# Six GpSimd steps of a fused attention and channel-mix kernel wait for a VectorE step

## The chip, the cores and the metric

One core of one Trainium2 chip runs the kernel. The metric is the device time of one execution in microseconds (us). Inside the core five engines work side by side: TensorE (PE, the matmuls; its weight loads are listed as PEld), VectorE (DVE), ScalarE (ACT), GpSimd (POOL), and SyncE (SP), which here only issues DMAs. Each engine works through its own queue in program order; an instruction starts when the ones ahead of it are through and the semaphores that it waits for have come.

## The reference

The inputs q, k and v are 4 batches x 4 heads x 1088 positions x 32 numbers. The first part is an attention with polynomial features, linear in the sequence:

```
def phi(x):
    a = np.einsum('rd,bhsd->bhsr', S1, x)
    b = np.einsum('rd,bhsd->bhsr', S2, x)
    return np.einsum('bhsi,bhsj->bhsij', a, b).reshape(*x.shape[:-1], r * r)
q_p, k_p = (phi(q), phi(k))
kv = np.einsum('bhsf,bhsd->bhfd', k_p, v)
z = np.sum(k_p, axis=2)
num = np.einsum('bhsf,bhfd->bhsd', q_p, kv)
den = np.einsum('bhsf,bhf->bhs', q_p, z)[..., None] + 1e-06
```

Its result num / den, with the heads side by side, is x (4 x 1088 x 128). The second part mixes each position with the one before it and runs a two-layer network with a gate:

```
xk = mu_k * x + (1.0 - mu_k) * x_prev
xr = mu_r * x + (1.0 - mu_r) * x_prev
k = np.maximum(xk @ w_k, 0.0)
v = k * k @ w_v
r = 1.0 / (1.0 + np.exp(-(xr @ w_r)))
return (r * v).astype(np.float32)
```

Here r = 8 features each (64 products), and the inner width of the network is 1024.

## The kernel before

The kernel is a set of small functions, each of which issues one step of the work, and a string, `ORDER`, in which the steps are written out by hand in the order in which they are issued. The loop at lines 622 to 628 takes the entries one after the other. An entry such as `qp.2.0.V` names the function (`qp`), its arguments (batch 2, half 0) and the engine (V VectorE, G GpSimd, A ScalarE; P also means VectorE, with an operand read in PSUM); `@` gives the PSUM banks. Entries without an engine letter are TensorE steps, except those whose function fixes the engine. Since each engine works in order, `ORDER` fixes the queue of every engine. Waits between engines are put in by the framework, from the tiles that a step reads and writes and from the buffers that it takes over; two steps on different engines that share no tile are free to run at the same time.

The work of one batch, in the names that the prediction uses (lines are those of the step's instruction; many copies go through the helper `copy`, lines 200 and 202):

- Attention, key side: `turn` (L259, L262) transposes k and q in 32x32 blocks on VectorE; `kproj` projects on TensorE, `abev` copies the result out, `kp` (L296) forms the 64 products, `kvmm` (L325) multiplies them with v, `kvev` copies out (tile kvs), `kvt` (L343) transposes on TensorE, `kvtev` copies out.
- Attention, query side: `abw` (L384) projects q, `abwev` copies out; `pw` (L404) and `den` (L411, L412) form the denominator; `an` (L420) divides one factor by it; `qp` (L429) forms the 64 products of each position, 128x1152 in half 0 and 128x1024 in half 1, both inputs from SBUF when the letter is V or G; `qd` (L438) transposes them on VectorE; `xmm` (L511) and `xt` (L477) multiply with kv; `xev` and `xtev` copy x out, and `xs` copies 31 numbers per row so that each position finds the one before it.
- Channel mix, on groups g of 512 columns of positions (g = 2 x batch + half; g = 8 holds the 64 left over of every batch row): `xk` (L527) and `xkt` (L530) mix on VectorE with one input in PSUM; `f1.g.c` (L551) is the first layer, c one quarter of the inner width; `relu` (L559) on ScalarE writes k1; `sq` (L574) squares it into k2 (128x1024 bf16, both inputs the same SBUF tile); `f2.g.c` (L584) is the second layer, summed over c. `xh` and `xht` cast x to bf16 for the gate: `rr` (L597) multiplies, `sig` (L605) takes the sigmoid on ScalarE, `fin` (L610) multiplies gate and result on VectorE and issues the output DMAs. `wset` (L208) and `cset` prepare weights, `zz` (L173) are matmuls on zeros.

PSUM has eight banks, handed out in `ORDER`; a TensorE step also waits until the reader of what stood in its bank before is through. So `f1.5.0@12` waits for `fin.2`, which reads `f2.2`'s sums in bank 2, and `xmm.3.2@4567` for `relu.4.2` (banks 5 and 6).

Of the kernel before, what the change touches and what calls it, by code (L numbers as in the profile page):

```python
# [34 lines left out]
ORDER = """  # L35
turn.k.0.0.V smm.0@0 cset.0 turn.k.0.1.V zz.5@7 kproj.0.1@0 abev.0.1.A kproj.0.0@1 turn.q.0.1.V cset.4.G abev.0.0.V
smm.1@2 cset.1.V cset.2.G turn.q.0.0.V kp.0.0.G zz.1@7 zmm.0@3 zev.0.A zz.2@7 wmm.0 wsq.0 kp.0.1.P zz.2@7 abw.0.0@2
abwev.0.0.A pw.0.0.P den.0.0 an.0.0.V abw.0.1@3 abwev.0.1.A pw.0.1.G kvmm.0@2 kvev.0.A zz.2@7 kvt.0 turn.k.1.2.V
zz.3@7 kproj.1.1@0 den.0.1 qp.0.0.G an.0.1.G qp.0.1.P abev.1.1.A kp.1.1.G kproj.1.0@1 abev.1.0.A kvtev.0.A qt.0.0@45
qtev.0.0.A turn.q.1.2.V wset.0.G qtt.0@2 qt.0.1@67 qttev.0.A zmm.1@3 zev.1.A qtev.0.1.A zz.2@5 wmm.1 xmm.0.0@45 xt.0  # L40
xtev.0.A xev.0.0.A xmm.0.1@67 kp.1.0.P xev.0.1.A wsq.1 abw.1.1@3 cset.3 xs.0.V xk.0.0 xh.0.0.A xk.0.1 xh.0.1.A
abw.1.0@1 abwev.1.1.V xkt.0 abwev.1.0.A f1.0.3@45 wset.2.G relu.0.3.A f1.0.0@67 wset.1.G relu.0.0.A pw.1.2.G f1.1.3@23
f1.1.2@01 rr.0@4 sig.0.A relu.1.2.A relu.1.3.A turn.k.2.2.V kproj.2.1@5 den.1.2 kproj.2.0@6 abev.2.0.A turn.q.2.2.V
f1.1.0@01 kvmm.1@4 abev.2.1.V zmm.2@2 turn.k.3.2.V kproj.3.0@3 kp.2.0.P kproj.3.1@5 relu.1.0.A zev.2.A wmm.2 f1.0.1@01
sq.0.0.A kvev.1.A kvt.1 abev.3.1.V abev.3.0.A sq.0.3.G relu.0.1.A wsq.2 f1.0.2@67 relu.0.2.A abw.2.0@3 an.1.2.G
qp.1.0.G qp.1.1.G kvtev.1.A rr.1@0 qd.1.0.V qd.1.1.V sig.1.A sq.0.1.A abwev.2.0.V abw.2.1@1 abwev.2.1.A xmm.1.2@4567
turn.q.3.2.V kp.3.1.G zmm.3@3 xt.1@1 xev.1.1.V sq.0.2.A xtev.1.V kp.3.0.G zev.3.V f2.0.0@0 f2.0.1 xev.1.0.A wmm.3
xs.1.G sq.1.2.A f2.0.2 sq.1.3.A xkt.1 f2.0.3 xk.1.0 pw.2.2.G xk.1.1 f1.1.1@12 relu.1.1.A f1.2.0@45 relu.2.0.A wsq.3
fin.0.S f1.3.1@67 den.2.2 sq.1.1.V an.2.2.V abw.3.0@0 abw.3.1@1 relu.3.1.A f1.3.2@23 f1.2.1@45 sq.2.0.A sq.1.0.V
relu.2.1.A xht.0.G kp.2.1.G kvmm.2@6 kvmm.3@7 abwev.3.0.A qp.2.0.V sq.3.1.V xh.1.0.G kvev.2.V qp.2.1.G abwev.3.1.V  # L50
kvev.3.V kvt.2 relu.3.2.A f1.3.0@45 relu.3.0.A pw.3.2.G qd.2.0.V qd.2.1.V f1.3.3@01 relu.3.3.A kvtev.2.V sq.3.0.V
f2.1.0@2 f2.1.1 kvt.3 kvtev.3.A f1.2.3@34 relu.2.3.A sq.2.3.V xh.1.1.G f2.1.2 den.3.2 f1.2.2@01 relu.2.2.A f2.1.3
sq.3.2.A xmm.2.2@3456 xev.2.0.A sq.2.1.G xt.2@0 fin.1.S rr.2@1 xtev.2.V xs.2.G xh.2.0.G an.3.2.G f2.3.0@7 xev.2.1.V
sq.2.2.A sig.2.A xk.2.0 xkt.2 xk.2.1 qp.3.0.V f2.2.0@2 qd.3.0.V f2.3.1 f2.2.1 f1.4.0@01 f2.2.2 f1.4.1@34 sq.3.3.A
relu.4.0.A f2.2.3 fin.2.S relu.4.1.A f1.4.3@56 relu.4.3.A qp.3.1.G sq.4.0.G rr.3@0 sig.3.A f1.5.3@34 f2.3.2 f2.3.3
f1.4.2@56 qd.3.1.V relu.5.3.A fin.3.S sq.4.3.V relu.4.2.A sq.4.2.V f1.5.0@12 sq.4.1.V rr.4@0 sig.4.A xt.3@3 xh.2.1.V
xtev.3.A sq.5.3.V xs.3.V relu.5.0.A sq.5.0.G xmm.3.2@4567 f2.4.0@0 xev.3.0.A xev.3.1.A xkt.3 f1.5.1@12 f2.4.1 f2.4.2
xk.3.0 xk.3.1 rr.5@3 xht.3.V relu.5.1.A sig.5.A f1.5.2@12 sq.5.1.V f2.4.3 xh.3.0.V relu.5.2.A sq.5.2.V f1.6.3@45
relu.6.3.A fin.4.S xh.3.1.V f2.5.0@3 f1.6.0@67 f2.5.1 sq.6.3.V relu.6.0.A f1.6.1@12 relu.6.1.A f2.5.2 f1.6.2@45
relu.6.2.A f2.5.3 f1.7.1@67 relu.7.1.A sq.6.0.V fin.5.S sq.6.1.V sq.6.2.V f1.7.0@01 relu.7.0.A sq.7.0.V f2.6.0@2  # L60
xht.1.V sq.7.1.V f1.8.0@45 relu.8.0.A rr.7@3 f2.6.1 f1.7.3@67 relu.7.3.A sq.7.3.V sq.8.0.V f2.6.2 f1.7.2@01 relu.7.2.A
f2.6.3 sq.7.2.V f1.8.1@45 relu.8.1.A rr.6@6 sig.6.A f2.7.0@7 f1.8.3@01 relu.8.3.A f2.7.1 sq.8.1.V f1.8.2@45 relu.8.2.A
f2.7.2 sig.7.A f2.7.3 xht.2.G rr.8@0 fin.6.S sq.8.3.V sig.8.A sq.8.2.V f2.8.0@4 f2.8.1 fin.7.S f2.8.2 f2.8.3 fin.8.SAG
"""


# [592 lines left out]
```

## Time and profile before

| | us |
|---|---|
| median of 3 runs | 87.15 |
| fastest and slowest of them | 86.06, 87.16 |
| the profiled execution | 86.39 |
| its span in the profile | 84.6 |

In the rows that the prediction shows, the first number is the start in us from the begin of the span, the second the duration in us; then come the engine, the line, the operation, the tiles written and read, the shapes, the number of instructions merged in the row (x1, x2), and in brackets how long the engine had stood idle before the row and what it had waited for. An instruction on VectorE is listed from about 0.07 us before the one ahead of it ends, so starts lie closer than durations. The span in 40 slices of 2.1 us, busy tenths of each:

```profile
PE   5989999999999989999985999997985999999200
DVE  5269677896999899389999999999999999699400
ACT  0602041488999997699991999999764699999000
POOL 5032949899399999288642842997084000000300
PEclk9999999999999999999999999999999999999995
```

The granted TensorE clock is at 9 tenths or more until the last slice. GpSimd has work mainly in the first three quarters; VectorE and TensorE are listed as busy almost throughout, and a step that has started and is held up is listed as busy.

### The profile page before, as it was taken

What the parts mean: (1) busy time and instruction counts of PE and PEld (TensorE: products, weight loads), DVE (VectorE), ACT (ScalarE), POOL (GpSimd) and SP (SyncE); (2) the same over time, 40 slices, a digit from 0 to 9 for tenths busy, and PEclk for the clock granted to TensorE, in tenths of its full rate; (3) what the DMA queues carried; (4) which work ended last, traced back from release to release, by engine and by line L of the source; (5) the groups of instructions that cost most, each with busy time, mean ns of one, the idle gap of its engine ahead of it and who ended that gap; (6) DMA issues with size and microseconds to landing.
All of it is one profiled execution on the core that took longest, in us unless ns stands there. A gap on an engine that the chain in (4) does not pass through costs nothing.

```text
span 84.6 us, 3600 instructions
## 1 busy us (share of the span) xinstructions
PE 73.8 (87%) x1558; PEld 54.1 (64%) x1558; DVE 69.7 (82%) x121; ACT 58.7 (69%) x87; POOL 44.5 (53%) x54
## 2 busy tenths in 40 slices
PE   5989999999999989999985999997985999999200
PEld 2257786977598857496673879674644777899100
DVE  5269677896999899389999999999999999699400
ACT  0602041488999997699991999999764699999000
POOL 5032949899399999288642842997084000000300
PEclk9999999999999999999999999999999999999995
DMA  0999999999999600001210000400350004400550
GB/s 1 285 313 246 348 385 226 277 366 354 337 197 231 156 1 8 8 0 31 74 31 8 0 8 0 124 12 0 95 143 18 0 0 124 124 8 11 141 139 22
DMA packets 10132, 10.26 MB, mean 121 GB/s; under 512 B 1170, under 2 KB 7540, under 8 KB 10116
## 3 DMA queue, kind: packets, MB, share of 16 engines
q1 hardware_dynamic: 10016, 9.97, 42.0%
q8 instruction: 12, 0.20, 1.0%
q0 software_dynamic: 32, 0.03, 0.2%
q10 hardware_dynamic: 68, 0.03, 0.2%
q14 instruction: 4, 0.03, 0.1%
HBM read 7.80 MB, written 2.23 MB: 119 GB/s over the span
## 4 chain that ended last, share of the span: by engine, by line
PE 39%; DVE 25%; issue 20%; DMA 3%; POOL 3%; ACT 2%; POOLq 1%; SPq 0%; DVEq 0%
PE ps L551 6%; PE ps L272 5%; DVE k L574 5%; DVE qpT L438 4%; DVE qp L429 4%; PE ps L173 4%; PE ps L384 3%; DMA k<-in_k_dram 3%; PE ps L325 3%; DVE k L610 3%; PE ps L278 3%; DVE xk L527 2%; POOL k L574 2%; PE ps L511 2%; PE ps L367 2%
## 5 line engine op out<-in xcount | busy, mean ns | idle before, releaser
L559 ACT ACTIVATE k<-ps 128x1024 bf16<-128x1024 f32 (+1 forms) x36 | 33.2, 1006 | 2.0 <-PE ps L551 1.9
L584 PEld LDWEIGHTS <-k 128*128 128x128 bf16 x272 | 16.8, 98 | 5.4 <-DVE k L574 1.6
L584 PE MATMUL ps<-wv,k 128*128 128x128 bf16 x272 | 19.1, 219 | 1.1 <-DVE k L574 1.1
L551 PE MATMUL ps<-xk,wk 128*128 128x512 bf16 x64 | 17.8, 379 | 0.7 <-DVE k L610 0.6
L574 DVE TENSOR_TENSOR k<-k 128x1024 bf16<-128x1024 bf16 (+1 forms) x23 | 16.4, 749 | 0.8 <-ACT k L559 0.8
L429 POOL TENSOR_TENSOR qp<-an,abw 128x1024 f32<-128x1024 f32 (+1 forms) x5 | 10.6, 2127 | 1.4 <-DVE an L420 1.2
L296 POOL TENSOR_TENSOR kp<-ab 128x1024 f32<-128x1024 f32 (+1 forms) x5 | 10.6, 2140 | 0.3 <-ACT ab L200 0.3
L574 POOL TENSOR_TENSOR k<-k 128x1024 bf16<-128x1024 bf16 x4 | 8.9, 2214 | 3.4 <-ACT k L559 3.0
L572 ACT ACTIVATE k<-k 128x1024 bf16<-128x1024 bf16 x9 | 9.6, 1074 | 0.0
L617 POOL DMA_DIRECT2D out_dram<-rt x1 | 0.7, 712 | 15.2 <-DVE rt L610 15.2
L173 PE MATMUL ps<-zero 128*128 128x512 bf16 x22 | 7.5, 455 | 1.0 <-DVE warm L155 1.0
L551 PEld LDWEIGHTS <-wk 128*128 128x128 bf16 x72 | 6.0, 100 | 2.8 <-issue 0.3
L438 DVE STREAM_TRANSPOSE qpT<-qp 128x1152 f32<-128x1152 f32 (+1 forms) x6 | 7.6, 1289 | 0.0
L605 ACT ACTIVATE k<-ps 128x512 f32<-128x512 f32 x8 | 5.1, 636 | 2.8 <-PE ps L597 2.8
L527 DVE SCALAR_TENSOR_TENSOR xk<-ps,rat,qx 128x512 bf16<-128x512 f32 x8 | 5.7, 744 | 0.4 <-ACT qx L200 0.4
L200 ACT COPY ab<-ps 128x320 f32<-128x320 f32 (+1 forms) x5 | 2.1, 417 | 5.7 <-PE ps L278 2.9
L429 DVE TENSOR_TENSOR qp<-an,abw 128x1152 f32<-128x1152 f32 x2 | 5.9, 2970 | 0.0
L262 DVE STREAM_TRANSPOSE qT<-qx 128x1088 f32<-128x1088 f32 (+2 forms) x5 | 5.3, 1068 | 0.7 <-DMA qx<-in_q_dram 0.7
L511 PE MATMUL ps<-qpT,kvt 32*32 32x256 f32 x192 | 5.5, 386 | 0.1
L610 DVE TENSOR_TENSOR k<-ps,k 128x512 f32<-128x512 f32 x8 | 5.4, 670 | 0.1
L597 PEld LDWEIGHTS <-x 128*128 128x128 bf16 x64 | 4.0, 98 | 2.2 <-POOL k L574 0.9
L404 POOL TENSOR_TENSOR pw<-abw 128x272 f32<-128x272 f32 (+1 forms) x4 | 2.8, 695 | 5.0 <-DVE abw L202 2.8
(107 smaller groups left out, 123.8 us busy)
## 6 DMA issues: line engine op xcount, KB each, us to landing
out_dram<-k SPq DMA_DIRECT2D x32, 64.0 KB, 1.7
k<-in_k_dram SPq DMA_DIRECT2D x6, 272.0 KB, 5.4
qx<-in_q_dram SPq DMA_DIRECT2D x6, 272.0 KB, 6.3
v<-in_v_dram SPq DMA_DIRECT2D x8, 144.0 KB, 6.7
v<-in_v_dram SPq DMA_DIRECT2D x8, 128.0 KB, 4.6
wk_f<-in_moe_w_k_dram SPq DMA_DIRECT2D x1, 512.0 KB
wv_f<-in_moe_w_v_dram SPq DMA_DIRECT2D x1, 512.0 KB, 7.7
k<-in_k_dram SPq DMA_DIRECT2D x1, 288.0 KB, 2.8
```

What stands on the lines that cost most here:

```text
L173: nc.tensor.matmul(PS[:, banks[0], :], zero[:], _ap(zero[:], [[0, 4], [1, P]]), skip_group_check=True)
L296: e.tensor_mul(o[:], _ap(a_, list(a_.ap[1:]) + [[0, R]]), _ap(b_, [list(b_.ap[1]), [0, R], list(b_.ap[2])]))
L429: e.tensor_mul(o[:, :s1 - s0], _ap(a_, list(a_.ap[1:]) + [[0, R]]), _ap(b_, [list(b_.ap[1]), [0, R], list(b_.ap[2])]))
L438: nc.vector.transpose(sb["qpT", b][:].rearrange("p s y a -> p (s y a)")[:, F * s0:F * s1], sb["qp", b, g][:].rearrange("p s i j -> p (s i ...
L511: nc.tensor.matmul(o[32 * h:32 * h + 32, c, :], sb["kvt", b][y, f, 32 * h:32 * h + 32], m, start=(f == 0), stop=(f == 1), skip_group_check ...
L527: nc.vector.scalar_tensor_tensor(like(o[:], b), ps["x", b, g], rat[:], like(xslots(b, g, 0), b), op0=MUL, op1=ADD)
L551: nc.tensor.matmul(h[:, c, :], wk[:, 2 * cp + c].rearrange("p y f -> p (y f)"), x, skip_group_check=True)
L559: nc.scalar.activation(o[:, :, :size(g)], h, RELU)
L572: nc.scalar.activation(o[:, :, :n], k1[:, :, :n], SQUARE)
L574: (nc.gpsimd if eng == "G" else nc.vector).tensor_mul(o[:, :, :n], k1[:, :, :n], k1[:, :, :n])
L584: nc.tensor.matmul(o[:, i * P:i * P + P], k2[:, c, i * P:i * P + P], wv[:, 2 * cp + c, :], start=(cp == 0 and c == 0 and i == 0), stop=(cp ...
L610: nc.vector.tensor_mul(o, ps["o", g][:, :n], o)
```

## The change

The order of the steps is the same, entry by entry. Six entries of GpSimd steps get a suffix, `^` and the name of a VectorE step that stands ahead of them in the order: from then on the first GpSimd instruction of that entry waits for the last VectorE instruction of the named one. None of the six reads what the named step writes.

| entry (GpSimd) | waits for (VectorE) |
|---|---|
| `pw.0.1.G` (L404) | `an.0.0.V` (L420) |
| `wset.2.G` (L208, the first of two) | `xs.0.V` (L202) |
| `xh.1.0.G` (L202) | `sq.3.1.V` (L574) |
| `sq.2.1.G` (L574) | `sq.2.3.V` (L574) |
| `qp.3.1.G` (L429) | `qp.3.0.V` (L429) |
| `sq.5.0.G` (L574) | `xs.3.V` (L202) |

The queue of GpSimd from the third of them on is, in order: `xht.0`, `kp.2.1`, `xh.1.0`, `qp.2.1`, `pw.3.2`, `xh.1.1`, `sq.2.1`, `xs.2`, `xh.2.0`, `an.3.2`, `qp.3.1`, `sq.4.0`, `sq.5.0`, `xht.2`, and one output DMA at the end.

The string `ORDER` is wrapped anew; its words differ in these six suffixes alone. Three of the lines, and the loop:

```
-kvev.3.V kvt.2 relu.3.2.A f1.3.0@45 relu.3.0.A pw.3.2.G qd.2.0.V qd.2.1.V f1.3.3@01 relu.3.3.A kvtev.2.V sq.3.0.V
...
+sq.3.1.V xh.1.0.G^sq.3.1.V kvev.2.V qp.2.1.G abwev.3.1.V kvev.3.V kvt.2 relu.3.2.A f1.3.0@45 relu.3.0.A pw.3.2.G
...
+sq.2.3.V xh.1.1.G f2.1.2 den.3.2 f1.2.2@01 relu.2.2.A f2.1.3 sq.3.2.A xmm.2.2@3456 xev.2.0.A sq.2.1.G^sq.2.3.V xt.2@0
...
+    ends = {}
+    traced = nc.cur_bb.bb.instructions
     for entry in ORDER.split():
         task, _, banks = entry.partition("@")
+        task, _, tie = task.partition("^")
         name, *args = task.split(".")
         args = [int(a) if a.isdigit() else a for a in args]
         if banks:
             args.append([int(i) for i in banks])
+        done = len(traced)
         does[name](*args)
+        mine = traced[done:]
+        for i in mine:
+            if i.engine == mybir.EngineType.DVE:
+                ends[task] = i.name
+        if tie:
+            first = next(i for i in mine if i.engine == mybir.EngineType.Pool)
+            tc.add_manual_dep(first, ends[tie], mybir.DependencyInfo(mybir.DependencyClass.Sync,
+                                                                     mybir.DependencyReason.DATA), reason="tie")
```

More of the change, by code (lines that the diff above doesn't have):

```diff
@@ L37 @@
 smm.1@2 cset.1.V cset.2.G turn.q.0.0.V kp.0.0.G zz.1@7 zmm.0@3 zev.0.A zz.2@7 wmm.0 wsq.0 kp.0.1.P zz.2@7 abw.0.0@2
[L38 to L50, printed above, removed]
-kvev.3.V kvt.2 relu.3.2.A f1.3.0@45 relu.3.0.A pw.3.2.G qd.2.0.V qd.2.1.V f1.3.3@01 relu.3.3.A kvtev.2.V sq.3.0.V
@@ L52 @@
[L52 to L61, printed above, removed]
@@ L62 @@
-f2.6.3 sq.7.2.V f1.8.1@45 relu.8.1.A rr.6@6 sig.6.A f2.7.0@7 f1.8.3@01 relu.8.3.A f2.7.1 sq.8.1.V f1.8.2@45 relu.8.2.A
-f2.7.2 sig.7.A f2.7.3 xht.2.G rr.8@0 fin.6.S sq.8.3.V sig.8.A sq.8.2.V f2.8.0@4 f2.8.1 fin.7.S f2.8.2 f2.8.3 fin.8.SAG
+abwev.0.0.A pw.0.0.P den.0.0 an.0.0.V abw.0.1@3 abwev.0.1.A pw.0.1.G^an.0.0.V kvmm.0@2 kvev.0.A zz.2@7 kvt.0
+turn.k.1.2.V zz.3@7 kproj.1.1@0 den.0.1 qp.0.0.G an.0.1.G qp.0.1.P abev.1.1.A kp.1.1.G kproj.1.0@1 abev.1.0.A
+kvtev.0.A qt.0.0@45 qtev.0.0.A turn.q.1.2.V wset.0.G qtt.0@2 qt.0.1@67 qttev.0.A zmm.1@3 zev.1.A qtev.0.1.A zz.2@5
@@ new lines @@
+wmm.1 xmm.0.0@45 xt.0 xtev.0.A xev.0.0.A xmm.0.1@67 kp.1.0.P xev.0.1.A wsq.1 abw.1.1@3 cset.3 xs.0.V xk.0.0 xh.0.0.A
+xk.0.1 xh.0.1.A abw.1.0@1 abwev.1.1.V xkt.0 abwev.1.0.A f1.0.3@45 wset.2.G^xs.0.V relu.0.3.A f1.0.0@67 wset.1.G
+relu.0.0.A pw.1.2.G f1.1.3@23 f1.1.2@01 rr.0@4 sig.0.A relu.1.2.A relu.1.3.A turn.k.2.2.V kproj.2.1@5 den.1.2
+kproj.2.0@6 abev.2.0.A turn.q.2.2.V f1.1.0@01 kvmm.1@4 abev.2.1.V zmm.2@2 turn.k.3.2.V kproj.3.0@3 kp.2.0.P
+kproj.3.1@5 relu.1.0.A zev.2.A wmm.2 f1.0.1@01 sq.0.0.A kvev.1.A kvt.1 abev.3.1.V abev.3.0.A sq.0.3.G relu.0.1.A wsq.2
@@ new lines @@
+f1.0.2@67 relu.0.2.A abw.2.0@3 an.1.2.G qp.1.0.G qp.1.1.G kvtev.1.A rr.1@0 qd.1.0.V qd.1.1.V sig.1.A sq.0.1.A
+abwev.2.0.V abw.2.1@1 abwev.2.1.A xmm.1.2@4567 turn.q.3.2.V kp.3.1.G zmm.3@3 xt.1@1 xev.1.1.V sq.0.2.A xtev.1.V
+kp.3.0.G zev.3.V f2.0.0@0 f2.0.1 xev.1.0.A wmm.3 xs.1.G sq.1.2.A f2.0.2 sq.1.3.A xkt.1 f2.0.3 xk.1.0 pw.2.2.G xk.1.1
+f1.1.1@12 relu.1.1.A f1.2.0@45 relu.2.0.A wsq.3 fin.0.S f1.3.1@67 den.2.2 sq.1.1.V an.2.2.V abw.3.0@0 abw.3.1@1
+relu.3.1.A f1.3.2@23 f1.2.1@45 sq.2.0.A sq.1.0.V relu.2.1.A xht.0.G kp.2.1.G kvmm.2@6 kvmm.3@7 abwev.3.0.A qp.2.0.V
@@ new lines @@
+sq.3.1.V xh.1.0.G^sq.3.1.V kvev.2.V qp.2.1.G abwev.3.1.V kvev.3.V kvt.2 relu.3.2.A f1.3.0@45 relu.3.0.A pw.3.2.G
+qd.2.0.V qd.2.1.V f1.3.3@01 relu.3.3.A kvtev.2.V sq.3.0.V f2.1.0@2 f2.1.1 kvt.3 kvtev.3.A f1.2.3@34 relu.2.3.A
+sq.2.3.V xh.1.1.G f2.1.2 den.3.2 f1.2.2@01 relu.2.2.A f2.1.3 sq.3.2.A xmm.2.2@3456 xev.2.0.A sq.2.1.G^sq.2.3.V xt.2@0
+fin.1.S rr.2@1 xtev.2.V xs.2.G xh.2.0.G an.3.2.G f2.3.0@7 xev.2.1.V sq.2.2.A sig.2.A xk.2.0 xkt.2 xk.2.1 qp.3.0.V
+f2.2.0@2 qd.3.0.V f2.3.1 f2.2.1 f1.4.0@01 f2.2.2 f1.4.1@34 sq.3.3.A relu.4.0.A f2.2.3 fin.2.S relu.4.1.A f1.4.3@56
@@ new lines @@
+relu.4.3.A qp.3.1.G^qp.3.0.V sq.4.0.G rr.3@0 sig.3.A f1.5.3@34 f2.3.2 f2.3.3 f1.4.2@56 qd.3.1.V relu.5.3.A fin.3.S
+sq.4.3.V relu.4.2.A sq.4.2.V f1.5.0@12 sq.4.1.V rr.4@0 sig.4.A xt.3@3 xh.2.1.V xtev.3.A sq.5.3.V xs.3.V relu.5.0.A
+sq.5.0.G^xs.3.V xmm.3.2@4567 f2.4.0@0 xev.3.0.A xev.3.1.A xkt.3 f1.5.1@12 f2.4.1 f2.4.2 xk.3.0 xk.3.1 rr.5@3 xht.3.V
+relu.5.1.A sig.5.A f1.5.2@12 sq.5.1.V f2.4.3 xh.3.0.V relu.5.2.A sq.5.2.V f1.6.3@45 relu.6.3.A fin.4.S xh.3.1.V
+f2.5.0@3 f1.6.0@67 f2.5.1 sq.6.3.V relu.6.0.A f1.6.1@12 relu.6.1.A f2.5.2 f1.6.2@45 relu.6.2.A f2.5.3 f1.7.1@67
@@ L64 @@
+relu.7.1.A sq.6.0.V fin.5.S sq.6.1.V sq.6.2.V f1.7.0@01 relu.7.0.A sq.7.0.V f2.6.0@2 xht.1.V sq.7.1.V f1.8.0@45
+relu.8.0.A rr.7@3 f2.6.1 f1.7.3@67 relu.7.3.A sq.7.3.V sq.8.0.V f2.6.2 f1.7.2@01 relu.7.2.A f2.6.3 sq.7.2.V f1.8.1@45
+relu.8.1.A rr.6@6 sig.6.A f2.7.0@7 f1.8.3@01 relu.8.3.A f2.7.1 sq.8.1.V f1.8.2@45 relu.8.2.A f2.7.2 sig.7.A f2.7.3
+xht.2.G rr.8@0 fin.6.S sq.8.3.V sig.8.A sq.8.2.V f2.8.0@4 f2.8.1 fin.7.S f2.8.2 f2.8.3 fin.8.SAG
 """
```

## The prediction

> **What bounds the kernel now.** I read the page first: the busy shares and the chain that ended last. Then the timelines of VectorE (DVE), GpSimd (POOL) and TensorE (PE) beside each other, to see which step an engine stands still for.
>
> ```profile
> PE 73.8 (87%) x1558; PEld 54.1 (64%) x1558; DVE 69.7 (82%) x121; ACT 58.7 (69%) x87; POOL 44.5 (53%) x54
> PE 39%; DVE 25%; issue 20%; DMA 3%; POOL 3%; ACT 2%; POOLq 1%; SPq 0%; DVEq 0%
> ```
>
> No engine is full over the span, so the stages decide. The chain goes over PE and DVE. The TensorE timeline has its idle time in brackets:
>
> ```profile
> 41.70 2.54 PE L325 MATMUL ps<-kp,v 128*32 128x64 f32 x144
> 45.40 0.44 PE L343 MATMUL ps<-ident,kvs 128*128 128x128 f32 x2 [1.16 <-DVE kvs L202]
> 59.06 0.38 PE L551 MATMUL ps<-xk,wk 128*128 128x512 bf16 x1 [0.62 <-DVE k L610]
> 60.21 2.02 PE L511 MATMUL ps<-qpT,kvt 32*32 32x256 f32 x64
> 64.29 1.07 PE L584 MATMUL ps<-wv,k 128*128 128x128 bf16 x16 [1.07 <-DVE k L574]
> 65.58 0.61 PE L597 MATMUL ps<-wr,x 128*128 128x128 bf16 x8 [0.23 <-DVE XT L530]
> 66.03 0.59 PE L551 MATMUL ps<-xk,wk 128*128 128x512 bf16 x2
> ```
>
> From 41.70 on TensorE is full but for four stops, all ended by VectorE: 1.16 + 0.62 + 1.07 + 0.23 = 3.08 us. Each is longer than the bracket says: the L597 row lasts 0.61 us by its modelled end, but the next one starts 0.45 after it, so some 0.16 us of issue time is hidden in front of each bracket; 4 x 0.16 = 0.64, in all 3.7 us. That is the most that TensorE can give back here, if VectorE were early at all four. From 65.58 on it has no further stop, so whatever moves that row moves the end.
>
> Why is VectorE late? Its own rows (between them it does not idle) beside those of GpSimd:
>
> ```profile
> 39.51 0.91 DVE L574 TENSOR_TENSOR k<-k 128x1024 bf16<-128x1024 bf16 x1
> 40.34 0.43 DVE L420 TENSOR_TENSOR an<-abw,den 128x272 f32<-128x272 f32 x1
> 40.69 0.68 DVE L574 TENSOR_TENSOR k<-k 128x1024 bf16<-128x1024 bf16 x1
> 41.29 3.11 DVE L429 TENSOR_TENSOR qp<-an,abw 128x1152 f32<-128x1152 f32 x1
> 44.33 0.68 DVE L574 TENSOR_TENSOR k<-k 128x1024 bf16<-128x1024 bf16 x1
> 46.06 1.36 DVE L438 STREAM_TRANSPOSE qpT<-qp 128x1152 f32<-128x1152 f32 x1
> 48.79 1.93 DVE L574 TENSOR_TENSOR k<-k 128x1024 bf16<-128x1024 bf16 x2
> 52.69 0.74 DVE L527 SCALAR_TENSOR_TENSOR xk<-ps,rat,qx 128x512 bf16<-128x512 f32 x1
> 54.20 2.83 DVE L429 TENSOR_TENSOR qp<-an,abw 128x1152 f32<-128x1152 f32 x1
> 57.05 1.38 DVE L438 STREAM_TRANSPOSE qpT<-qp 128x1152 f32<-128x1152 f32 x1
> 60.66 3.57 DVE L574 TENSOR_TENSOR k<-k 128x1024 bf16<-128x1024 bf16 x3
> 65.18 0.17 DVE L202 COPY qx<-qx 128x31 f32<-128x31 f32 x1
> ```
>
> ```profile
> 39.23 0.64 POOL L202 CAST x<-qx 128x544 bf16<-128x544 f32 x1
> 40.85 2.34 POOL L429 TENSOR_TENSOR qp<-an,abw 128x1024 f32<-128x1024 f32 x1 [0.98 <-DVE an L420]
> 45.95 0.77 POOL L404 TENSOR_TENSOR pw<-abw 128x272 f32<-128x272 f32 x1 [2.76 <-DVE abw L202]
> 47.67 1.90 POOL L574 TENSOR_TENSOR k<-k 128x1024 bf16<-128x1024 bf16 x1 [0.38 <-PE ps L584]
> 52.24 0.21 POOL L202 COPY qx<-qx 128x31 f32<-128x31 f32 x1 [2.67 <-DVE qx L202]
> 53.85 1.96 POOL L429 TENSOR_TENSOR qp<-an,abw 128x1024 f32<-128x1024 f32 x1
> 55.76 3.01 POOL L574 TENSOR_TENSOR k<-k 128x1024 bf16<-128x1024 bf16 x1
> 61.63 2.06 POOL L574 TENSOR_TENSOR k<-k 128x1024 bf16<-128x1024 bf16 x1 [2.86 <-ACT k L559]
> ```
>
> The same square (L574) has a plain length and a long one. All VectorE squares between 38 and 66 us, grouped by the tile that they write, minimum, median, maximum:
>
> ```profile
> L574 DVE TENSOR_TENSOR k<-k x9: 674/680/2384, 39.5 to 64.6; 128x1024 bf16<-128x1024 bf16 x9
> ```
>
> Plain is 0.68 (0.61 from one start to the next, 40.69 to 41.29). The long ones all lie beside a GpSimd row, and their ends fit one reading: a VectorE step with both inputs in SBUF stands still until the GpSimd step has ended, and does its whole work after it. GpSimd's qp.2.1 ends at 40.85 + 2.34 = 43.19, VectorE's qp.2.0 at 41.29 + 3.11 = 44.40: 1.21 apart. In the second pair 53.85 + 1.96 = 55.81 and 54.20 + 2.83 = 57.03: 1.22 apart. Two rows of 3.11 and 2.83 have the same remainder. It goes the other way too: GpSimd's square sq.4.0 at 55.76 lasts 3.01, and 57.03 to 58.77 is nearly its own 1.90 of row 47.67.
>
> **The change part by part.** No step is added, removed or put elsewhere in the order, no DMA is touched; six GpSimd steps get a wait on the VectorE step that they ran beside. I take 0.08 us for a hand-over (VectorE's an ends at 40.34 + 0.43 = 40.77, the GpSimd step that waited for it starts at 40.85).
>
> First the two early ones (pw.0.1 behind an.0.0; wset.2 behind xs.0).
>
> ```profile
> 11.90 0.47 POOL L404 TENSOR_TENSOR pw<-abw 128x128 f32<-128x128 f32 x1 [0.92 <-ACT abw L200]
> 12.62 2.18 POOL L429 TENSOR_TENSOR qp<-an,abw 128x1152 f32<-128x1152 f32 x1 [0.24 <-DVE an L420]
> 15.46 1.96 POOL L296 TENSOR_TENSOR kp<-ab 128x1024 f32<-128x1024 f32 x1 [0.30 <-ACT ab L200]
> 22.55 0.77 POOL L404 TENSOR_TENSOR pw<-abw 128x272 f32<-128x272 f32 x1 [1.29 <-ACT abw L200]
> ```
>
> ```profile
> 12.07 0.46 DVE L420 TENSOR_TENSOR an<-abw,den 128x144 f32<-128x144 f32 x1
> 20.01 0.30 DVE L202 COPY qx<-qx 128x31 f32<-128x31 f32 x1 [0.43 <-ACT qx L200]
> ```
>
> Pw.0.1 now starts when an.0.0 has ended, and qp.0.0 is queued behind it. Alone, an.0.0 (144 elements) takes at most the 0.43 that 272 take at 40.34, so it ends between 12.3 and 12.5, pw.0.1 ends 0.5 later at 12.8 to 13.0, and qp.0.0 starts 0.2 to 0.4 after its 12.62. Two idle stretches cover that: 0.30 on GpSimd before 15.46 and 0.43 on VectorE before 20.01, both ended by ScalarE. I take 0; without the cover it would be 0.4 at most. Wset.2 waits until about 20.3, GpSimd loses about 0.7, and the 1.29 of idle before 22.55 takes it; without it, 0.7. I take 0.
>
> Third, xh.1.0 behind sq.3.1. VectorE's sq.1.1 falls from 0.91 to 0.68 (the cast beside it, 39.23 to 39.87, is gone) and qp.2.0 from 3.11 to about 1.25: 2.1 us, so sq.3.1 ends at about 42.9 rather than 45.01. Queued behind xh.1.0 on GpSimd is qp.2.1, which so far started at 40.85: xh.1.0 at 43.0 to 43.6, qp.2.1 to 45.6 at its plain 1.96. Its reader is the second transpose at L438. VectorE does not keep all 2.1 us: kvev.3 needs the matmuls of 41.70, which end at 44.24. So kvev.2 at 43.0, kvev.3 at 44.3, the first transpose at 44.6 (46.06 before), the second at 45.9, after its input. VectorE is 1.45 early, and the first stop of TensorE is gone: kvt.2 at 44.24 instead of 45.40.
>
> Fourth, sq.2.1 behind sq.2.3.
>
> ```profile
> 46.30 1.94 ACT L559 ACTIVATE k<-ps 128x1024 bf16<-128x1024 f32 x2 [1.85 <-PE ps L551]
> 48.38 1.05 ACT L559 ACTIVATE k<-ps 128x1024 bf16<-128x1024 f32 x1
> 57.52 1.96 ACT L559 ACTIVATE k<-ps 128x1024 bf16<-128x1024 f32 x2
> 66.23 0.60 ACT L605 ACTIVATE k<-ps 128x512 f32<-128x512 f32 x1 [1.89 <-PE ps L597]
> ```
>
> ScalarE follows TensorE (idle before 46.30), 1.2 early; relu.2.3 (48.38) then ends at 48.2, sq.2.3 at 48.9 where it ended at 50.72, with 0.64 of blocking gone (1.93 to 1.29). GpSimd: sq.2.1 at 49.0 to 50.9, then xs.2 behind it to 51.1. Xs.2 is the cost: xk.2.0 on VectorE reads what it copies, and would be ready at 50.9. It comes at 51.15, so 1.55 early and not 1.8.
>
> Fifth, qp.3.1 behind qp.3.0. VectorE: qp.3.0 at 52.65 to 53.95 in place of 57.03, so 3.1 early. GpSimd: qp.3.1 54.0 to 56.0, sq.4.0 behind it to 57.9 (58.77 before). The step fin.2 at L610, which frees the PSUM bank for row 59.06, moves from 58.36 to 55.2. The second transpose needs qp.3.1 and would be ready at 55.8: it waits 0.2. TensorE's 59.06 stop goes; the matmuls of 60.21 now wait for the bank that ScalarE's second step of 57.52 frees (59.48 before, 58.3 after): about 0.3 of stop is left there, and they start at 58.3, 1.9 early.
>
> Sixth, sq.5.0 behind xs.3. The three squares of 60.66 take 1.9 instead of 3.57 and end at 59.7 rather than 64.23, so the 1.07 stop goes. ScalarE's evictions after the matmuls then lead: xkt.3 can run at 61.45, TensorE's row 65.58 starts at 62.0, that is 3.55 early. Sq.5.0 itself runs on GpSimd from about 60.9 to 62.8, beside steps with an input in PSUM (xkt, xk); its reader f2.5.0 comes after 63.8. ScalarE's 66.23 row moves as TensorE's does, and its 1.89 of idle is used up.
>
> **Sum.** By TensorE: 3.08 + 0.64 - 0.3 = 3.4; by following the steps: 3.55. I take 3.5 us. The profiled execution took 86.39 us (span 84.6 and 1.8 around it); it becomes 82.9. The median of the runs shown, 87.15, is 0.8 higher, so 83.6.
>
> A rule of the Trainium skill could speak against this. The page "SBUF — State Buffer", section "Who interferes with whom", says that issue order and not the op's shape decides which of the two engines is blocked, for the whole instruction. By it each tied GpSimd step would now be first, and could block the next VectorE step with two SBUF inputs. Whether it does depends on the rows: behind sq.3.1 the next such step is sq.3.0 at 47.4, and GpSimd is done at 47.0 (qp.2.1 to 45.6, then 0.77 of row 45.95 and a cast of 0.64); behind qp.3.0 it is sq.4.3 at 57.75, against sq.4.0 until 57.9: 0.1 us. By the rule with a GpSimd step half a microsecond later the sum would be 0.5 to 1 us smaller; I keep 3.5, and the case stands below.
>
> **The rivals.**
> *POOL's queue comes late.* Xs.2 is behind sq.2.1. So far GpSimd idled 2.67 before it (row 52.24). If relu.2.3 does not come earlier, sq.2.3 ends near 50.0, sq.2.1 at 52.0, xs.2 at 52.2, and xk.2.0 gains 0.45 and not 1.55: 1.1 less, 84.7. Against it: ScalarE's row 46.30 was waiting for TensorE.
> *The block only moves.* Sq.4.0 blocks the three squares as sq.5.0 did. It costs when qp.3.1 starts late: the stops at 64.29 and 65.58 (1.07 + 0.23 + 0.32) come back, gain 1.9, time 85.25. Against it: the second transpose needs qp.3.1 and both fin steps stand ahead of the squares.
> *ScalarE holds the rest.* If its order is full after 46.30, only the first stop is gained (1.2): 85.95. Against it: 1.89 idle before 66.23.
> *Slower: the long VectorE rows are their own length.* No 128x1152 product with both inputs in SBUF runs alone in this trace. Then the waits come on top: sq.3.1 ends at 45.01, qp.2.1 at 47.65 (the second transpose 0.3 late), sq.2.1 from 50.8 to 52.7, xs.2 to 53.0 (xk.2.0 0.3 more), qp.3.1 to 59.6 (0.1 more): 0.7 slower, 87.85. It decides if a VectorE qp stays above 2.8. Against it: the two remainders of 1.2.
> *The waits do nothing*, as something already held them: 87.15. Against it: each tied step starts before the VectorE step ends.
>
> **How the numbers follow.** Chances: forecast 0.60; late queue 0.15; moved block 0.08; ScalarE 0.09; own length 0.05; nothing 0.03. The prediction is the forecast's, 83.6. Low end: the fastest run shown (86.06) less the 3.7 that TensorE can give back at most, 82.4. High end: the moved block, 85.3. That leaves out the last three cases, 0.17. Within 2% is about what a measurement of this kernel can tell from no change; 2% below 87.15 is 85.4. Faster: forecast, late queue and half of the moved block, 0.79. Same: the other half, ScalarE, nothing and most of the slower case, 0.18. Slower by over 2%: 0.03, for an own-length case worse than worked out.
>
> **What would show it.** Right: VectorE's two qp rows (L429, 128x1152) at 1.2 to 1.35; no L574 row on VectorE above 0.8 between 39 and 66; GpSimd's squares at 1.9 each; TensorE's idle before kvt.2 and f2.4.1 gone; the stretch from the L597 row on to the end as long as before, 3.5 earlier. Wrong: a VectorE qp row still near 3; an idle row of VectorE at xk (L527) or at L438 that GpSimd ends; a VectorE square of 2 us beside sq.4.0; a new idle stretch of TensorE ended by ScalarE.

## The result, and the profile after

| | median us | range, runs | before, median on the same chip | ratio to before, 95% interval |
|---|---|---|---|---|
| the changed kernel | 82.43 | 82.02 to 83.14, 4 | 87.16 | 0.951, 0.938 to 0.963 |

The change makes the kernel 4.9% faster. Medians are of all runs; ratios and their intervals, here and below, leave out the runs that took over 1.5% longer than the fastest of their kernel. The profiled executions stand at 86.39 us (before) and 82.68 us (after), spans 84.6 and 80.9. Line numbers of the kernel after are one higher than before.

First TensorE in the timeline of the kernel after, the rows that answer to the four stops, with `f1.4.0` (52.68) and `f2.4.0` (59.96), which are needed further below (start, duration, engine, line, operation; idle time in front in brackets, where there was any):

```profile
42.16 2.54 PE L326 MATMUL ps<-kp,v 128*32 128x64 f32 x144
44.63 0.44 PE L344 MATMUL ps<-ident,kvs 128*128 128x128 f32 x2
...
52.68 0.59 PE L552 MATMUL ps<-xk,wk 128*128 128x512 bf16 x2
...
56.64 1.03 PE L552 MATMUL ps<-xk,wk 128*128 128x512 bf16 x4
57.51 0.61 PE L598 MATMUL ps<-wr,x 128*128 128x128 bf16 x8
...
58.29 1.73 PE L512 MATMUL ps<-qpT,kvt 32*32 32x256 f32 x64
59.96 0.62 PE L585 MATMUL ps<-wv,k 128*128 128x128 bf16 x8
...
60.85 1.06 PE L585 MATMUL ps<-wv,k 128*128 128x128 bf16 x16
61.74 0.61 PE L598 MATMUL ps<-wr,x 128*128 128x128 bf16 x8
```

No row has a bracket: all four stops are gone. From `kvmm.2` (L325, now L326) to `rr.5` (the last row), which is the stretch in which the change acts, it was 65.58 - 41.70 = 23.88 us and is 61.74 - 42.16 = 19.58: 4.30 us less. I call this the stage below. The profiled span is shorter by only 3.7, since this execution reached `kvmm.2` 0.46 later; it already ran 0.58 behind at GpSimd's first `kp` (start 8.59 before, 9.17 after), ahead of every added wait. Behind `rr.5` the kernel takes as long as before: GpSimd's output DMA was issued 14.02 us after it both times (65.58 to 79.60, 61.74 to 75.76).

VectorE after, its rows in the places of the long ones:

```profile
41.48 1.35 DVE L430 TENSOR_TENSOR qp<-an,abw 128x1152 f32<-128x1152 f32 x1
...
45.10 2.49 DVE L439 STREAM_TRANSPOSE qpT<-qp 128x1152 f32<-128x1152 f32 x2
...
48.70 0.69 DVE L575 TENSOR_TENSOR k<-k 128x1024 bf16<-128x1024 bf16 x1 [0.21 <-ACT k L560]
...
51.03 0.69 DVE L203 COPY qx<-ps 128x512 f32<-128x512 f32 x1 [0.18 <-ACT qx L201]
51.64 0.74 DVE L528 SCALAR_TENSOR_TENSOR xk<-ps,rat,qx 128x512 bf16<-128x512 f32 x1
...
53.15 1.34 DVE L430 TENSOR_TENSOR qp<-an,abw 128x1152 f32<-128x1152 f32 x1
...
55.83 0.65 DVE L611 TENSOR_TENSOR k<-ps,k 128x512 f32<-128x512 f32 x1
...
58.31 1.87 DVE L575 TENSOR_TENSOR k<-k 128x1024 bf16<-128x1024 bf16 x3
...
62.84 1.00 DVE L575 TENSOR_TENSOR k<-k 128x1024 bf16<-128x1024 bf16 x1
```

The two products take 1.35 and 1.34 where they took 3.11 and 2.83, the three squares 1.87 in place of 3.57. One square is longer than it was: `sq.5.1` at 62.84 takes 1.00, where it took 0.68 before (at 66.93). GpSimd after:

```profile
43.56 0.64 POOL L203 CAST x<-qx 128x544 bf16<-128x544 f32 x1 [3.82 <-DVE k L575]
...
49.54 1.89 POOL L575 TENSOR_TENSOR k<-k 128x1024 bf16<-128x1024 bf16 x1 [2.13 <-DVE k L575]
51.38 0.21 POOL L203 COPY qx<-qx 128x31 f32<-128x31 f32 x1
...
54.58 1.96 POOL L430 TENSOR_TENSOR qp<-an,abw 128x1024 f32<-128x1024 f32 x1 [1.66 <-DVE qp L430]
56.49 1.89 POOL L575 TENSOR_TENSOR k<-k 128x1024 bf16<-128x1024 bf16 x1
61.40 1.89 POOL L575 TENSOR_TENSOR k<-k 128x1024 bf16<-128x1024 bf16 x1 [3.01 <-DVE qx L203]
```

GpSimd now idles in front of the tied steps, 3.82, 2.13, 1.66 and 3.01 us, and none of them is stretched: the square of 3.01 us before is back at 1.89. The idle time costs nothing: between 41 and 63 us no idle time of another engine is ended by GpSimd. A meeting that is left is that of `sq.5.0` (61.40 to 63.29) with `sq.5.1`, which ends at 63.84, 0.55 after it; by the 14.02 us above it does not move the end.

### The profile page after: what moved, and what is told of

The parts are those of the page before. It is cut to its first block, busy times and chain, and to the rows that moved or that the text cites. A ratio compares the mean times of both kernels' runs of the same rounds, so it can differ in the third digit from the quotient of the medians.

```text
span 80.9 us, 3603 instructions
## 1 busy us (share of the span) xinstructions
PE 73.3 (91%) x1558; PEld 54.5 (67%) x1558; DVE 64.2 (79%) x121; ACT 58.5 (72%) x87; POOL 42.6 (53%) x54
## 4 chain that ended last, share of the span: by engine, by line
PE 53%; issue 17%; DVE 13%; POOL 6%; ACT 3%; POOLq 1%
PE ps L174 9%; PE ps L552 7%; PE ps L326 6%; PE ps L385 5%; PE ps L273 5%; DVE qpT L439 3%; DVE k L575 3%; PE ps L279 3%; POOL qp L430 2%; PE ps L368 2%; POOL k L575 2%; PE ps L585 2%; PE ps L450 2%; PE ps L512 2%; DVE xk L528 2%
## 5 line engine op out<-in xcount | busy, mean ns | idle before, releaser
L585 PEld LDWEIGHTS <-k 128*128 128x128 bf16 x272 | 16.9, 98 | 4.1 <-issue 0.4
L585 PE MATMUL ps<-wv,k 128*128 128x128 bf16 x272 | 19.1, 219 | 0.0
L575 DVE TENSOR_TENSOR k<-k 128x1024 bf16<-128x1024 bf16 (+1 forms) x23 | 14.2, 647 | 0.9 <-ACT k L560 0.9
L575 POOL TENSOR_TENSOR k<-k 128x1024 bf16<-128x1024 bf16 x4 | 7.6, 1893 | 5.3 <-DVE qx L203 3.0
L174 PE MATMUL ps<-zero 128*128 128x512 bf16 x22 | 8.2, 494 | 1.0 <-DVE warm L156 1.0
L326 PEld LDWEIGHTS ps<-kp,v 128*32 128x32 f32 x288 | 4.3, 110 | 1.3 <-issue 0.4
L326 PE MATMUL ps<-kp,v 128*32 128x64 f32 x288 | 4.9, 220 | 0.1
L385 PE MATMUL ps<-SQ,qT 128*32 128x96 f32 x192 | 5.0, 247 | 0.0
L512 PE MATMUL ps<-qpT,kvt 32*32 32x256 f32 x192 | 5.0, 385 | 0.0
```

The lines of the kernel that those rows point to most:

```text
L174: nc.tensor.matmul(PS[:, banks[0], :], zero[:], _ap(zero[:], [[0, 4], [1, P]]), skip_group_check=True)
L326: nc.tensor.matmul(o[32 * h:32 * h + 32, :], vin[b][:, h, m, :], sb["kp", b, j][:, 4 * (m - KG[j][0]) + h].rearrange("p i j -> p (i j)"), ...
L385: nc.tensor.matmul(d, qT[b % 2][:, 16 * g + (quad(t) + c if TURN[b] == "O" else 4 * c + t), :], SQ[b][:], skip_group_check=True, tile_posi ...
L575: (nc.gpsimd if eng == "G" else nc.vector).tensor_mul(o[:, :, :n], k1[:, :, :n], k1[:, :, :n])
L585: nc.tensor.matmul(o[:, i * P:i * P + P], k2[:, c, i * P:i * P + P], wv[:, 2 * cp + c, :], start=(cp == 0 and c == 0 and i == 0), stop=(cp ...
```

## The experiments

The theory: a VectorE step with both inputs in SBUF and a GpSimd step that reads SBUF exclude each other; VectorE, late by that, held TensorE at four places, and the gain is these stops. A wait's number is its place in the table of the change, from 1 to 6. The rivals are in the expectations, each with its run. In the table the stage gain is from one profiled execution of each kernel, `kvmm.2` to `rr.5` against 23.88 of before; for the three marked * it is counted from `kvt.2` (L343) on, 20.18 before, since nothing of the stage is changed ahead of that in them, and in e1 and e8 the matmuls of `kvmm` ran in two pieces. The stage leaves out what varies ahead of it: `kvmm.2` started between 41.15 (e8) and 43.46 us (e1) in these executions. Where nothing in it is changed it repeats, with 23.88 in p1 as in before, and 20.18 from `kvt.2` on in e1. Each "before" is the kernel before on the same chip.

| kernel | waits kept | median us | before | ratio, 95% interval | stage gain us |
|---|---|---|---|---|---|
| e1 | 1, 2 | 87.30 | 86.95 | 1.004, 1.000 to 1.009 | 0.00* |
| e2 | 3 | 86.54 | 86.95 | 0.993, 0.988 to 0.998 | 0.74 |
| e7 | 5 | 85.52 | 86.80 | 0.976, 0.965 to 0.987 | 1.30* |
| e8 | 6 | 84.76 | 86.80 | 0.976, 0.968 to 0.983 | 1.64* |
| e3 | 5, 6 | 84.16 | 86.95 | 0.975, 0.968 to 0.982 | 2.87 |
| e4 | 1, 2, 3, 5, 6 | 83.00 | 86.95 | 0.957, 0.949 to 0.966 | 3.61 |
| e6 | 3, 4, 5, 6 | 82.98 | 86.80 | 0.954, 0.945 to 0.963 | 4.0 |
| the change | all | 82.43 | 87.16 | 0.951, 0.938 to 0.963 | 4.30 |

**The early waits alone (e1).**

```
-sq.2.1.G^sq.2.3.V   (and the third, fifth and sixth in the same way)
+sq.2.1.G
```

> Only the two early waits (pw.0.1 behind an.0.0, wset.2 behind xs.0). Theory (a VectorE step with both inputs in SBUF and a GpSimd step exclude each other, and the gain is the late TensorE stops that VectorE ended): no change, within 0.4 us of before, since GpSimd's 0.30 and 1.29 us of idle and VectorE's 0.43 take the 0.1 to 0.4 that qp.0.0 comes late. The rest of the profile as before: VectorE qp rows of 3.1 and 2.8. Rival (the early waits cost what GpSimd loses): 0.3 to 0.7 us slower.

The ratio's interval touches 1: they bring nothing, and cost at most what the interval allows, 0.8 us. It doesn't tell 0.35 us from none, so the rival is not excluded by this run alone.

**The third alone (e2).**

```
-qp.3.1.G^qp.3.0.V   (and all others but the third)
+qp.3.1.G
```

> Only xh.1.0 behind sq.3.1. Theory: the first TensorE stop goes (1.16 + 0.16), the later ones stay, so 1.2 to 1.5 us faster; VectorE's qp.2.0 about 1.35, its qp.3.0 still about 2.8 and three squares still about 3.5. Rival (what VectorE saves goes to the end undiminished): 2.1 us faster. Rival (nothing is gained until the last stop goes): within 0.5 us of before.

Faster, but by 0.4 in the medians and 0.74 in the stage, less than the 1.2 to 1.5 expected. By the medians alone the rival of under 0.5 us would stand; the stage, and the first stop, which is gone, speak against it. The rows of VectorE and GpSimd in this kernel say why:

```profile
41.37 1.35 DVE L430 TENSOR_TENSOR qp<-an,abw 128x1152 f32<-128x1152 f32 x1
...
47.72 2.60 DVE L575 TENSOR_TENSOR k<-k 128x1024 bf16<-128x1024 bf16 x2
```

```profile
47.28 1.90 POOL L575 TENSOR_TENSOR k<-k 128x1024 bf16<-128x1024 bf16 x1
```

The product is free, and the first stop went. But VectorE came early to the two squares `sq.3.0` and `sq.2.3`, and GpSimd's `sq.2.1` still started at the old place: the squares now take 2.60, not 1.93. What the third wait gains is half lost at the next meeting. TensorE shows it as a stop that was not there before, 0.31 us ended by VectorE's `fin.1` ahead of L585 at 51.71.

**All but the fourth (e4).**

```
-sq.2.1.G^sq.2.3.V
+sq.2.1.G
```

> All waits but the fourth (sq.2.1 behind sq.2.3). Theory: sq.2.1 starts near 47.7 and holds sq.3.0 and sq.2.3 back by 0.6 to 1 us in all; xs.2 is no longer behind it. TensorE's f1.4.0 waits for VectorE's xkt.2 then: 0.2 to 0.6 us slower than the full change, so 3.2 to 4 us faster than before. Rival (the fourth wait costs as much through xs.2 as it saves): as fast as the full change or faster.

Here too the squares take 2.60 us, and TensorE has the 0.30 us stop in front of L585. The stage gains 3.61, 0.69 less than with all waits. So the fourth wait is worth 0.7 once the third is there, and its cost through `xs.2` does not eat it. The rival falls on the stage; the two medians, from different chips, would not tell it alone.

**The fifth and sixth (e3), and each alone (e7, e8).**

```
-xh.1.0.G^sq.3.1.V   (e3: also the first, second and fourth)
+xh.1.0.G
```

> Only qp.3.1 behind qp.3.0 and sq.5.0 behind xs.3. Theory: the TensorE stops before f1.5.0, f2.4.1 and rr.5 go (0.62 + 1.07 + 0.23 + 3 x 0.16 = 2.4), the first stays: 2.2 to 2.8 us faster. Rival (VectorE's saving undiminished, 1.6 + 1.7): 3.3 us faster. Rival (the last stops alone decide): as fast as the full change.

> Only qp.3.1 behind qp.3.0. Theory: the stop before f1.5.0 goes (0.62 + 0.16) and what xmm.3.2 lost inside its row of 2.02 (0.3); the squares beside sq.5.0 stay at 3.5 and the stops before f2.4.1 and rr.5 stay: 1.0 to 1.3 us faster. Rival (the gain appears only with the last wait): within 0.4 us of before.

> Only sq.5.0 behind xs.3. Theory: the stops before f2.4.1 and rr.5 go (1.07 + 0.23 + 2 x 0.16), those before stay: 1.5 to 1.8 us faster, and with the fifth wait alone it adds up to the two together (2.8 us). Rival (VectorE's saving counts undiminished, 1.65, and the fifth wait's too): 1.65 here but 1.5 there, 3.2 together.

The gains in the stage are where the theory had them (e3 is just above its 2.2 to 2.8), and there they add: 1.30 + 1.64 = 2.94 against 2.87 together, and 0.74 + 2.87 = 3.61, just what e4 shows for the third, fifth and sixth; the fourth makes it 4.30. Whole runs do not show this sum: by the ratios each alone is 2.4% faster and both together 2.5%, with intervals of 0.7 to 1.1% either way. So that they add rests on one profiled execution of each kernel. The rivals that let one wait decide fall, and so does the 3.2 together of VectorE's saving undiminished. One part of e7's expectation was wrong: the squares beside `sq.5.0` did not stay long, and the stop before `f2.4.1` went. VectorE, GpSimd and TensorE in e7:

```profile
60.84 1.87 DVE L575 TENSOR_TENSOR k<-k 128x1024 bf16<-128x1024 bf16 x3
62.64 2.13 DVE L203 CAST x<-qx 128x544 bf16<-128x544 f32 x1
```

```profile
62.57 1.90 POOL L575 TENSOR_TENSOR k<-k 128x1024 bf16<-128x1024 bf16 x1 [1.65 <-ACT k L560]
```

```profile
65.77 0.61 PE L598 MATMUL ps<-wr,x 128*128 128x128 bf16 x8 [1.39 <-DVE XT L531]
```

VectorE was early enough to be through with the squares when `sq.5.0` came, and then its next step, a cast with a single input, stood still: 2.13 us instead of the 0.43 it takes in the kernel after. The block had moved, and the stop before `rr.5` grew from 0.23 to 1.39. That is nearly the 1.07 + 0.23 that were expected to stay, so the time came out as expected with the loss at another step: that was luck. The Trainium skill, "SBUF — State Buffer", section "Who interferes with whom", says that copies and casts can enter a mode in which they contend with GpSimd for the ports that the two share. This row agrees.

**Without the early waits (e6).**

```
-pw.0.1.G^an.0.0.V
+pw.0.1.G
-wset.2.G^xs.0.V
+wset.2.G
```

> The full change without the two early waits. Theory: they neither cost nor bring anything (GpSimd's and VectorE's idle cover them), so as fast as the full change, within 0.4 us: from TensorE's kvmm.2 to rr.5 4.3 us less than before. Rival (qp.0.0 0.3 late costs 0.3): 0.3 to 0.5 us faster than the full change.

0.954 against 0.951 of the full change, with intervals of about 0.01 either way: as fast, as far as these runs can tell, and not faster, as the rival had it. In its stage (42.33 to 62.18) it has a stop of 0.30 us within `kvmm` that no other engine ended, and that e1, which has the early waits, shows too; without it, the gain would be about 4.3.

**The wait the other way round (e5, e9).** VectorE's products wait by semaphore for GpSimd's. If a blocked step does nothing while it is blocked, nothing should change.

```
-abwev.3.0.A qp.2.0.V sq.3.1.V xh.1.0.G kvev.2.V qp.2.1.G abwev.3.1.V
+abwev.3.0.A xh.1.0.G qp.2.1.G qp.2.0.V~qp.2.1.G sq.3.1.V kvev.2.V abwev.3.1.V
...
-qp.3.0.V f2.2.0@2
+qp.3.1.G qp.3.0.V~qp.3.1.G f2.2.0@2
...
-relu.4.3.A qp.3.1.G sq.4.0.G
+relu.4.3.A sq.4.0.G
```

(`~` marks a wait of the VectorE instruction for the named GpSimd step.)

> Without the six waits, but the two VectorE products wait the other way round: qp.2.0 on VectorE waits by semaphore until GpSimd's qp.2.1 has ended, and qp.3.0 until qp.3.1 has. Theory (the VectorE step does nothing until the GpSimd step has ended): as before, within 0.4 us, with VectorE rows of 1.35 and 1.2 to 1.9 us of idle in front of each in place of rows of 3.11 and 2.83. Rival (the two engines share the port and VectorE gets on more slowly meanwhile): the part done during the overlap is lost, 0.5 to 1.5 us slower.

It was slower, 88.81 against 86.80, ratio 1.018 (1.006 to 1.030), 2.01 in the stage: not as the theory had it, and in the stage more than the rival. VectorE and GpSimd in this kernel:

```profile
43.69 1.36 DVE L430 TENSOR_TENSOR qp<-an,abw 128x1152 f32<-128x1152 f32 x1 [1.85 <-POOL qp L430]
...
56.48 3.03 DVE L430 TENSOR_TENSOR qp<-an,abw 128x1152 f32<-128x1152 f32 x1 [1.55 <-POOL qp L430]
```

```profile
54.49 1.96 POOL L430 TENSOR_TENSOR qp<-an,abw 128x1024 f32<-128x1024 f32 x1
56.40 1.90 POOL L575 TENSOR_TENSOR k<-k 128x1024 bf16<-128x1024 bf16 x1
```

The first pair did as the theory says: the product starts when GpSimd is through and takes 1.36. It ends 1.39 after GpSimd (43.66) where it ended 1.21 after it in the kernel before, and TensorE's stop there is 1.33 instead of 1.16: that is the hand-over. In the second, GpSimd's next step `sq.4.0` started at 56.40, 0.08 before VectorE's product at 56.48, and held it until 58.30; 58.30 + 1.21 = 59.51, the row's end. In the kernel before, VectorE's product was already standing there when `qp.3.1` ended, and `sq.4.0` had to wait. To test this reading, `sq.4.0` was made to wait for the product:

```
-relu.4.3.A sq.4.0.G
+relu.4.3.A sq.4.0.G^qp.3.0.V
```

> The kernel before it (VectorE's two products wait by semaphore for GpSimd's), and GpSimd's sq.4.0 now waits for VectorE's qp.3.0, so that it can't begin in the 0.08 us between the end of qp.3.1 and the start of qp.3.0. Theory (that kernel lost its 2 us because sq.4.0 came in first and held qp.3.0 for a second GpSimd step): qp.3.0 falls from 3.03 to 1.35, TensorE's stop before f1.5.0 from 2.47 to 0.7, and the time comes back to that of before, 0.2 to 0.5 us above it. Rival (the semaphore wait itself loses what VectorE had done meanwhile): 1.2 to 2 us slower than before still.

The product is back at 1.36:

```profile
56.69 1.36 DVE L430 TENSOR_TENSOR qp<-an,abw 128x1152 f32<-128x1152 f32 x1 [1.56 <-POOL qp L430]
```

TensorE's stop before `f1.5.0` falls from 2.47 to 0.80, and the stage is 24.23 us (42.37 to 66.60), 0.35 longer than before, within what was expected. The median is 1.03 above that of before on its chip (87.95 against 86.92, ratio 1.014, 1.008 to 1.020): more than the stage explains, and between the theory's 0.2 to 0.5 and the rival's 1.2 to 2. The product's length and the stage decide for the theory. The rest lies outside the stage and was not settled; the profiled execution reached `kvmm.2` 0.67 later than before's.

**The pairs by themselves (p1).** Behind the end of the kernel before, nine pairs: a GpSimd step, some 0.3 us later a VectorE step.

```
+    bench = [
+        (None, two, 0),
+        (gtwo, None, 0),
+        (gtwo, two, 0),
+        (lambda: nc.gpsimd.tensor_copy(bm, bx[0]), two, 0),
+        (lambda: nc.gpsimd.memset(bm, 0.0), two, 0),
+        (gtwo, lambda: nc.vector.tensor_mul(bo, pf[:, :1152], bx[1]), 0),
+        (gtwo, lambda: nc.vector.transpose(bo, bx[0]), 0),
+        (gtwo, lambda: nc.vector.tensor_copy(bo, bx[0]), 0),
+        (gtwo, two, 1),
+    ]
```

> The order of before without the six waits, and behind its end nine pairs by themselves: a GpSimd step starts, some 0.3 us later a VectorE step, and the next pair waits for both. Theory (exclusion of a VectorE step with two SBUF inputs and a GpSimd step that reads SBUF): the VectorE product 128x1152 alone 1.3; beside a GpSimd product of 1.96 it ends 1.25 after that one; beside a GpSimd cast the same; beside a GpSimd memset, which reads nothing, 1.3; with one input in PSUM 1.3, as a transpose 1.3 beside the GpSimd product. A VectorE f32 copy SBUF to SBUF waits too, if it takes both ports. With VectorE first, GpSimd's product takes 1.95 more after VectorE's end. Rival (shared bandwidth): both rows longer than alone by the overlap, and neither starts after the other's end.

VectorE's and GpSimd's timelines behind the kernel's end, without the small steps between the pairs:

```profile
85.37 1.35 DVE L666 TENSOR_TENSOR v<-kT,kT 128x1152 f32<-128x1152 f32 x1
...
89.91 3.25 DVE L666 TENSOR_TENSOR v<-kT,kT 128x1152 f32<-128x1152 f32 x1
...
93.80 2.04 DVE L666 TENSOR_TENSOR v<-kT,kT 128x1152 f32<-128x1152 f32 x1
...
96.49 1.35 DVE L666 TENSOR_TENSOR v<-kT,kT 128x1152 f32<-128x1152 f32 x1
...
98.48 1.35 DVE L674 TENSOR_TENSOR v<-ps,kT 128x1152 f32<-128x1152 f32 x1
...
101.10 1.37 DVE L675 STREAM_TRANSPOSE v<-kT 128x1152 f32<-128x1152 f32 x1
...
103.72 2.66 DVE L676 COPY v<-kT 128x1152 f32<-128x1152 f32 x1
...
106.56 1.35 DVE L666 TENSOR_TENSOR v<-kT,kT 128x1152 f32<-128x1152 f32 x1
```

```profile
87.00 2.33 POOL L667 TENSOR_TENSOR v<-qT,qT 128x1024 f32<-128x1024 f32 x1 [6.78 <-DVE bs L680]
89.61 2.34 POOL L667 TENSOR_TENSOR v<-qT,qT 128x1024 f32<-128x1024 f32 x1 [0.28 <-DVE bs L693]
93.49 1.14 POOL L672 COPY v<-kT 128x1152 f32<-128x1152 f32 x1 [1.55 <-DVE bs L693]
96.17 1.06 POOL L673 MEMSET v<- 128x1152 f32 x1 [1.54 <-DVE bs L693]
...
103.42 2.34 POOL L667 TENSOR_TENSOR v<-qT,qT 128x1024 f32<-128x1024 f32 x1 [0.28 <-DVE bs L693]
106.72 3.38 POOL L667 TENSOR_TENSOR v<-qT,qT 128x1024 f32<-128x1024 f32 x1 [0.96 <-DVE bs L680]
```

Alone, VectorE's product takes 1.35 and GpSimd's 2.33 (not the 1.96 of the expectation, which a product of the kernel takes). Beside GpSimd's product it ends at 93.16, 1.21 after that one (91.95); beside a GpSimd copy at 95.84, 1.21 after 94.63. Beside a memset, which reads nothing, it takes 1.35; so does a VectorE product with one input in PSUM, and a transpose 1.37, both beside a GpSimd product (2.35 from 98.18 and 2.34 from 100.80). A VectorE f32 copy is 2.66 long and ends 0.62 after GpSimd's product, so it is blocked too; no run has this copy alone. And with VectorE first, GpSimd's product is the one that stretches, 3.38. Shared bandwidth would have lengthened both of a pair; where the two products meet, only the one that starts later is longer (3.25 beside 2.34, and 3.38 beside 1.35).

## Why the prediction was right, and where it fell short

The median of 82.43 lies in the range of 82.4 to 85.3, just above its lower end. That it lies inside is luck: the lower end is the fastest run less the 3.7 us that TensorE was said to be able to give back at most, and the stage alone gave 4.30. Step by step, "early" being counted from `kvmm.2`, which the profile after reached 0.46 later (so 45.40 - 44.63 + 0.46 = 1.23 for the first):

| step | forecast, us early | measured |
|---|---|---|
| `kvt.2` on TensorE, the first stop | 1.16 | 1.23 |
| first transpose, behind the third wait | 1.45 | 1.42 |
| `xk.2.0`, forecast by way of `sq.2.1` and `xs.2` | 1.55 | 1.51 |
| `fin.2`, behind the fifth wait | 3.16 | 2.99 |
| `xmm.3.2` (60.21 before) | 1.9 | 2.38 |
| `rr.5` (65.58 before) | 3.55 | 4.30 |

- *What bounds.* Right in kind: the four stops of TensorE are gone and the rest of the kernel moved with `rr.5`. But TensorE was not full outside the four; see the size below.
- *Why VectorE was late.* Right: 1.35, 1.34 and 1.87 in the rows, the isolated pairs, and e9, which gets the length of the plain product back with a semaphore. The rival that the long rows are their own length is out.
- *The early waits at nothing.* Right within what e1 and e6 can tell.
- *The third, fourth and fifth.* Right to 0.2 us. For `xk.2.0` the number is right and its reason is not: GpSimd was through with `xs.2` at 51.59, and VectorE's copy ahead of `xk.2.0` ended only at 51.72, after 0.18 us of waiting for ScalarE. So no cost through `xs.2` shows. And the prediction listed the gains side by side; e2 and e4 show that the third and the fourth hang together.
- *The size: 0.75 us too small in the stage.* The step that failed is the sum by TensorE: "From 41.70 on TensorE is full but for four stops", which makes 3.7 the most that it can give back, and "about 0.3 of stop is left there" for `xmm.3.2`. Two more rows of TensorE before, `rr.4` and `f2.4.0`, and the lengths from one start to the next in both kernels:

```profile
59.28 0.61 PE L597 MATMUL ps<-wr,x 128*128 128x128 bf16 x8
...
62.17 0.62 PE L584 MATMUL ps<-wv,k 128*128 128x128 bf16 x8
```

| TensorE, start to start | before | after | less |
|---|---|---|---|
| `kvmm.2` to `kvt.2`, first stop | 3.70 | 2.47 | 1.23 |
| `kvt.2` to `f1.4.0` | 8.27 | 8.05 | 0.22 |
| `f1.4.0` to `rr.4`, second stop | 5.61 | 4.83 | 0.78 |
| `rr.4` to `f2.4.0`, with `xmm.3.2` | 2.89 | 2.45 | 0.44 |
| `f2.4.0` to `f2.4.1`, third stop | 2.12 | 0.89 | 1.23 |
| `f2.4.1` to `rr.5`, fourth stop | 1.29 | 0.89 | 0.40 |

The four stops gave 3.64, close to the 3.72 of the forecast. No 0.3 of stop was left, and two stretches that hold no bracket gave 0.66 more. The 0.22 is a stop in front of `f1.4.0`: the chain of before that ended last comes to this row from VectorE's `xkt.2` (start, duration):

```profile
53.43 0.20 DVE XT L530
...
53.67 0.59 PE ps L551 x2
```

After, `xkt.2` is through (52.30 + 0.27) 0.11 before the row at 52.68, and the matmuls run on. The 0.44 is a stop at `xmm.3.2`, whose row is 1.73 long where it was 2.02. The waits of the weight loads between 59.9 and 62.5 us of before list it (total us, times, longest):

```profile
PEld ps L511 <- DVE k L610: 0.4, 1, 0.4
```

L610 there is `fin.3` (`f2.3.0@7` and `xmm.3.2@4567`: it frees bank 7), and its lateness goes back to the fifth pair: the row is 1.73 in e7 (fifth wait alone) and 2.02 in e8 (sixth alone), where the same entry of 0.4 is still listed. After the change it is not.
- *Against the profiled execution* the sum looked better than it was: 82.9 forecast, 82.68 measured, since the execution after started 0.46 late and so hid most of the 0.75. The medians differ by 4.7, where 3.5 was forecast.
- *The rule of the Trainium skill, weighed and priced at 0.1 us.* Right for the two places that were worked out: `sq.4.0` ended at 58.38 and the squares went through at 1.87. A third was overlooked: the prediction put `sq.5.0` beside steps with an input in PSUM, and it met `sq.5.1`, whose 1.00 is the square above 0.8 that was not to be there. That the one that starts first blocks the other showed where a wait was missing: in e2 (2.60), e7 (2.13) and e5 (3.03) GpSimd's row starts first, by 0.44, 0.07 and 0.08.
